# Two conversion calls after each of seven experts, raw tiles asked for at a call's end, and a branch that is announced

## The chip, the cores and the metric

The program runs on one core of a Trainium2 chip. The core has a tensor engine (PE, with its weight load PEld), a vector engine (DVE), a scalar engine (ACT), GpSimd (POOL), and SP, which mostly issues transfers. Each engine works through its own list of instructions in order; semaphores hold an instruction until what it needs is done, and whatever stands behind it on that engine waits too. The metric is the device time of one execution in microseconds (us): the median of several runs.

## The reference

Three blocks follow each other, on 2304 tokens of 512 values.

```
attn_out = _attn_ref(**attn_kwargs)            # 4 batches, 8 heads, 576 tokens, 64 values a head
x = _moe_ref(x=x, **moe_kwargs)                # 8 experts, each token goes to one or none
return _moe2_ref(x=x, **moe2_kwargs)           # gated block over all tokens

# _moe_ref, for each expert e
h = np.maximum(xc[mask] @ w1[e], 0.0)          # 512 -> 1024
y[mask] = gate_w[mask, None] * (h @ w2[e])     # 1024 -> 512
# _moe2_ref
gate = 1.0 / (1.0 + np.exp(-(x @ w_gate)))     # 512 -> 1536
return (gate * (x @ w_val) @ w_out)            # 1536 -> 512
```

The weights of the last block come as float64 and are turned into pairs of float32 (a high and a low part) on the chip.

## The kernel before

Attention takes the first 150 us or so. Then come the experts, then the gated block (`moe2_phase`) in six passes over five blocks of tokens, then a loop for tokens that found no place in an expert (`Overflow.run`). How many rounds that loop makes is known on the chip only; with these inputs it makes none. From the experts on, everything stands in `tc.manual_schedule()`: each engine keeps the order in which the code is written.

**One expert** (`moe_phase`) has four chunks. A chunk is `products1` on PE (L1165) into one of three banks, then ACT's `hh` (L1210) and DVE's `hl` (L1211), which empty the bank, then `wt.split`, which splits a chunk of the second weight into high and low (ACT L927, DVE `w_lo` L928), then `feed()`, which asks for more expert weights on SP's queue (L918). After the chunks come the turning of the next expert's tokens (`make_xt`, ACT L1105), some calls of `cv.tick()`, the second products for slots 128 to 255 (`second_half`), for slots 0 to 127 (`products2`, L933 to L935), the weighted sum (`add_up`, DVE) and the scatter back to memory (POOL). How many calls an expert has stands in `TICKS`.

**The conversion** (`Convert`, `cv`) turns 36 raw tiles of 512 KB into high and low parts, in six stages, each on an engine of its own:

- l: SP asks for a raw tile (L997). Three raw buffers, so tile i waits for b of tile i-3.
- a: ACT takes the absolute value of the high word (L1002).
- b: ACT takes its sign (L1040), DVE puts the bits together in three instructions (L1042, L1043, L1046).
- c: POOL multiplies by the sign (L1007).
- h: ACT rounds to the high part (L1014).
- o: DVE subtracts for the low part (L1017).

One call of `tick()` lets each stage go on by one tile, as far as the stage ahead of it was asked for. Nothing in a call waits; its instructions wait, on the engines, in the places where the calls put them.

```
def tick(self):
    for stage in "lohcba":
        self.go(stage)
```

Of the kernel before, what the change touches and what calls it, by code (L numbers as in the profile page):

```python
# [23 lines left out]
NJ = 5  # L24
CAP = 256
NEG = -1.0e30


class Attention:
# [48 lines left out]
    def setup(self):  # L78
# [8 lines left out]
        gp.affine_select(  # L87
            out=r, in_=r, pattern=[[0, 4], [1, 2 * W]], compare_op=ALU.is_ge, fill=NEG,
            base=-1, channel_multiplier=-1,
        )  # L90
        gp.affine_select(
            out=r, in_=r, pattern=[[0, 4], [-1, 2 * W]], compare_op=ALU.is_ge, fill=NEG,
            base=W, channel_multiplier=1,
# [14 lines left out]
        ve.tensor_copy(mp, m0)  # L108
        ve.memset(mp[0:32, :, 0:W], NEG)
        ve.tensor_copy(md, m0)  # L110
        ve.memset(md[:, :, 0:W], NEG)
        for h2 in range(2):
# [839 lines left out]
class Convert:  # L952
# [95 lines left out]
        )  # L1048

    def tick(self):  # L1050
        for stage in "lohcba":
            self.go(stage)

    def need(self, c, k):
# [3 lines left out]
def moe_phase(nc, tc, ctx, g, wt, pool_a, na, route, xd, cv, over, new_xt):  # L1058
# [1 line left out]

    TICKS = (0, 2, 3, 3, 3, 2, 2, 0)
    pool_b = ctx.enter_context(tc.tile_pool(name="m_w", bufs=1, reuse_waits="tile"))
    px = ctx.enter_context(tc.tile_pool(name="m_x", bufs=3, reuse_waits="tile"))
    p = ctx.enter_context(tc.tile_pool(name="m_p", bufs=2, reuse_waits="tile"))
# [30 lines left out]
    def make_xt(e):  # L1097
        xt = p.tile([128, 4, CAP], F32, tag="xt", name="xt")

        def turn(h):  # L1100
            for k in range(4):
                nc.tensor.transpose(xts[h][:, k], xg[e, h][:, 128 * k:128 * k + 128], g.ident)

        turn(0)
        nc.scalar.copy(out=xt[:, :, 0:128], in_=xts[0])  # L1105
        if e == 0:
            load_n(0)
        with tc.If(taken[e] > 128) as c:
            turn(1)
        with c.Else():  # L1110
            nc.tensor.matmul(xts[1][:, 0, 0:32], lhsT=g.one, rhs=g.one[:, 0:32], start=True, stop=True)
        nc.vector.tensor_copy(xt[:, :, 128:256], xts[1])
        return xt
# [89 lines left out]
    for e in range(E):  # L1203
        hs = []
        for c in range(4):
# [6 lines left out]
                out=lo, in0=ps, scalar=0.0, in1=hi.bitcast(F32), op0=ALU.max, op1=ALU.subtract  # L1212
# [7 lines left out]
            if c == 0 and e == E - 1:  # L1220
# [6 lines left out]
                for h in range(2):  # L1227
                    nc.gpsimd.tensor_scalar(
                        out=hot[:, h], in0=route.iota, scalar1=to[:, h:h + 1], scalar2=None, op0=ALU.is_equal
# [3 lines left out]
        if e + 1 < E:  # L1233
            xt = make_xt(e + 1)
        for _ in range(TICKS[e]):
            cv.tick()
# [62 lines left out]
def moe2_phase(nc, tc, ctx, g, cv, xt0, begun, acc, xd, out):  # L1299
# [79 lines left out]
    def sums_of(q, b, parts):  # L1379
        return [lambda a=a, t=t: s2(q, a, t, parts) for a, t in enumerate(tiles[b])]  # L1380

    def flush(left=0):
        while len(due) > left:
            due.pop(0)()
# [9 lines left out]
    for q in range(NP):  # L1394
# [3 lines left out]
        for b in order:  # L1398
# [13 lines left out]
                if q or b > 2:  # L1412
                    cv.tick()
            due += sums_of(q, b, parts)
    flush()


class Overflow:
# [163 lines left out]
def convert_sources(wg, wv, wo):  # L1582
    wg, wv, wo = (w.bitcast(I32) for w in (wg, wv, wo))
    srcs = []
    for i in range(FF // 256):
        for w in (wg, wv):
            for h in range(2):
                srcs.append(
                    w[256 * h:256 * h + 256, 512 * i:512 * i + 512].rearrange("(k p) f -> p k f", p=128)
                )  # L1590
        for h in range(2):
            srcs.append(
                wo[256 * i + 128 * h:256 * i + 128 * h + 128, :].rearrange("(k p) f -> p k f", p=128)
            )
    return srcs
# [26 lines left out]
@with_exitstack  # L1622
def fused_kernel(ctx: ExitStack, tc: tile.TileContext, q, k, v, w_skip, w_gate, w1, w2, wg, wv, wo, out):
    nc = tc.nc
    g = Globals()
    g.nc = nc
    const = ctx.enter_context(tc.tile_pool(name="const", bufs=1))
    dram = ctx.enter_context(tc.tile_pool(name="dram", bufs=1, space=DRAM))
    g.ident = const.tile([128, 128], F32, name="ident")
    make_identity(nc, g.ident)  # L1630
    xd = dram.tile([NT, DM], F32, name="xd")
    route = Route(nc, tc, ctx, g)
    g.one = route.one
    nc.vector.memset(g.one, 1.0)
    over = Overflow(nc, tc, ctx, g, route)
    na = 4
    pool_a = None
    cv = Convert(nc, convert_sources(wg, wv, wo))
    with tc.manual_schedule(), ExitStack() as right, ExitStack() as ctx_ps:
        with ExitStack() as c3:  # L1640
            wt = Weights(nc, tc, c3, w1, w2)
            with ExitStack() as c2:
                route.enter(c2)
                att = Attention(nc, tc, c2, g, q, k, v, w_skip, w_gate, xd)

                def extra(s):


                    nonlocal pool_a
                    if s == EXTRA:  # L1650
                        att.nat_ctx.close()
                        pool_a = ctx.enter_context(tc.tile_pool(name="w_a", bufs=na, side="right"))
                        wt.pool_x = pool_a
                    if s is None or s in LOADS:
                        n = wt.n1 + wt.n2
                        wt.load(2 if n < 18 and n // 4 % 2 else 1)

                attention_phase(att, route, extra)
                g.keep_busy(att.ps_t, "t", "ps_t", 5)
                route.finish_gates()  # L1660
            cv.enter(tc, right)
            pool_x = right.enter_context(tc.tile_pool(name="f_x", bufs=1, side="right"))
            with ExitStack() as c2:
                g.banks(ctx_ps.enter_context(tc.tile_pool(name="banks", bufs=1, space=PSUM, reuse_waits="tile")))
                over.enter(c2, g.spare)
                new_xt = lambda: tuple(
                    pool_x.tile([128, 4, 256], F32R, tag="xt" + n, name="fx" + n) for n in ("h", "l")
                )
                xt0, begun = moe_phase(nc, tc, c2, g, wt, pool_a, na, route, xd, cv, over, new_xt)
        with ExitStack() as c2:  # L1670
            pool_o = c2.enter_context(tc.tile_pool(name="f_o", bufs=1, reuse_waits="tile"))
            acc = [pool_o.tile([128, DM], F32, name=f"fo{t}") for t in range(NT // 128)]
            moe2_phase(nc, tc, c2, g, cv, xt0, begun, acc, xd, out)
    n = over.rounds()
    with ExitStack() as c2:
        over.run(n, c2, xd, w1, w2, cv, out)


# [27 lines left out]
```

## Time and profile before

| | us |
|---|---|
| three runs | 784.02, 778.4, 781.0 |
| median | 781.0 |
| profiled execution, its own time | 783.18 |
| its span in the profile | 781.5 |

Times of stretches below are counted in the span of the profiled execution. Its own time lies 1.7 us above its span and 2.2 us above the median of the three runs. The experts e0 to e6 end, for PE, at 169.5, 188.9, 211.1, 231.0, 252.1, 271.8 and 293.1 us; expert 7 and the start of the gated block run to 311, the gated block to 773.5, and the rest is the end of the program. PEclk is the clock granted to PE, 1.00 for 2.4 GHz and 0.50 for 1.2 GHz.

### The profile page before, as it was taken

To read this page: it belongs to the slowest core of one execution; us is meant where nothing else is said; L and a number is where in the kernel's file an instruction comes from. 1 tells how busy PE (TensorE), PEld (TensorE's weight loads), DVE (VectorE), ACT (ScalarE), POOL (GpSimd) and SP (SyncE) were. 2 spreads that over 40 slices of the span, in tenths; PEclk is the share of its full clock that TensorE was granted. 3 is DMA by queue.
4 is the path that set the end of the run, shared out by engine and by line. 5 is a ranking of instruction groups with operands and counts; after the bars stand their busy time and mean duration, and the time that the engine had idled before them with its cause. 6 is when DMAs were issued, how large, how long until landed. Compare 5 with 4: busy or idle time off the path is not lost.

```text
span 781.5 us, 13025 instructions
## 1 busy us (share of the span) xinstructions
PE 733.2 (94%) x4976; PEld 594.7 (76%) x4976; DVE 419.9 (54%) x880; ACT 306.9 (39%) x677; POOL 141.3 (18%) x163
## 2 busy tenths in 40 slices
PE   5999988779999779999999999999999999999995
PEld 3666665568988778978888888888888888888884
DVE  8767767556777757332234546534652653332332
ACT  4888884234545544333352323313321331111110
POOL 7224332312343233100011002000110010000000
PEclk9999999899999989999999999999999999999999
DMA  8799879595597762321012103100310000000122
GB/s 151 166 211 218 226 168 309 162 348 199 184 332 255 264 231 65 117 81 55 1 32 76 28 27 96 40 27 22 87 28 27 28 1 0 1 1 27 55 81 85
DMA packets 74997, 88.12 MB, mean 113 GB/s; under 512 B 15810, under 2 KB 52930, under 8 KB 74912
## 3 DMA queue, kind: packets, MB, share of 16 engines
q1 hardware_dynamic: 71008, 78.68, 34.9%
q0 software_dynamic: 2560, 6.15, 2.2%
q10 hardware_dynamic: 1344, 2.10, 0.7%
q8 instruction: 60, 0.98, 0.5%
q14 instruction: 25, 0.20, 0.1%
HBM read 75.52 MB, written 13.63 MB: 114 GB/s over the span
## 4 chain that ended last, share of the span: by engine, by line
PE 78%; DVE 7%; ACT 6%; DMA 5%; issue 3%; POOL 0%; SPq 0%; DVEq 0%; ACTq 0%; POOLq 0%
PE bank L942 26%; PE bank L947 13%; PE bank L935 8%; PE bank L933 8%; PE bank L934 8%; PE bank L1165 6%; DMA cv_raw<-in_moe_w_val_dram 2%; DMA cv_raw<-in_moe_w_gate_dram 2%; DVE w_lo L928 1%; ACT qTd L242 1%; PE ps_s L260 1%; ACT kTp L242 1%; ACT kTd L242 1%; PE ps_t L383 1%; DVE hl L1211 1%
## 5 line engine op out<-in xcount | busy, mean ns | idle before, releaser
L942 PE MATMUL bank<-fxh,w_hi 128*128 128x512 f32 (+1 forms) x480 | 177.7, 376 | 0.7 <-ACT fxh L1333 0.7
L942 PE MATMUL bank<-fxh,w_lo 128*128 128x512 f32 (+1 forms) x480 | 174.7, 370 | 0.0
L1359 DVE SCALAR_TENSOR_TENSOR th<-th,bank 128x512 f32<-128x512 f32 (+1 forms) x60 | 38.0, 634 | 184.3 <-PE bank L947 161.8
L947 PE MATMUL bank<-fxl,w_hi 128*128 128x512 f32 (+1 forms) x480 | 121.2, 372 | 0.0
L942 PEld LDWEIGHTS bank<-fxh,w_hi 128*128 128x128 f32 x480 | 90.3, 188 | 19.7 <-ACT fxh L1333 1.3
L1007 POOL TENSOR_TENSOR cv_x<-cv_x,cv_s 128x512 f32<-128x512 f32 x36 | 47.6, 1326 | 307.5 <-DVE cv_x L1046 282.2
L942 PEld LDWEIGHTS bank<-fxh,w_lo 128*128 128x128 f32 x480 | 90.3, 188 | 16.1
L947 PEld LDWEIGHTS bank<-fxl,w_hi 128*128 128x128 f32 x480 | 85.6, 188 | 17.5
L1165 PE MATMUL bank<-xt,w 128*128 128x128 f32 (+3 forms) x512 | 74.6, 309 | 16.6 <-issue 9.4
L1360 ACT CAST gh<-th 128x512 fp32r<-128x512 f32 (+1 forms) x60 | 34.7, 578 | 135.3 <-DVE th L1359 135.3
L1165 PEld LDWEIGHTS bank<-xt,w 128*128 128x128 f32 x512 | 71.8, 210 | 19.4 <-issue 9.6
L933 PE MATMUL bank<-w_hi,gh 128*128 128x512 f32 x216 | 85.6, 396 | 0.0
L934 PE MATMUL bank<-w_lo,gh 128*128 128x512 f32 x216 | 85.2, 395 | 0.0
L935 PE MATMUL bank<-w_hi,gl 128*128 128x512 f32 x216 | 85.2, 394 | 0.0
L1358 ACT ACTIVATE th<-bank 128x512 f32<-128x512 f32 (+1 forms) x60 | 33.3, 555 | 127.3 <-PE bank L947 126.8
L1375 DVE SCALAR_TENSOR_TENSOR fo<-bank,fo 128x512 f32<-128x512 f32 x90 | 61.6, 687 | 5.1 <-PE bank L935 3.0
L1361 DVE TENSOR_TENSOR gl<-th,gh 128x512 fp32r<-128x512 f32 (+1 forms) x60 | 39.2, 653 | 38.6 <-ACT gh L1360 38.6
L935 PEld LDWEIGHTS bank<-w_hi,gl 128*128 128x128 f32 x216 | 40.5, 188 | 9.6
L933 PEld LDWEIGHTS bank<-w_hi,gh 128*128 128x128 f32 x216 | 40.7, 188 | 9.2
L934 PEld LDWEIGHTS bank<-w_lo,gh 128*128 128x128 f32 x216 | 40.6, 188 | 9.1
L1002 ACT ACTIVATE cv_x<-cv_raw 128x512 f32<-128x512 f32 x36 | 24.2, 674 | 57.4 <-issue 32.8
L928 DVE TENSOR_TENSOR w_lo<-w,w_hi 128x1024 fp32r<-128x1024 f32 x32 | 41.3, 1292 | 3.7 <-ACT w_hi L927 3.4
(215 smaller groups left out, 1052.8 us busy)
## 6 DMA issues: line engine op xcount, KB each, us to landing
w<-in_moe_w_dram SPq DMA_DIRECT2D x62, 512.0 KB, 6.7
cv_raw<-in_moe_w_val_dram SPq DMA_DIRECT2D x12, 512.0 KB
cv_raw<-in_moe_w_out_dram SPq DMA_DIRECT2D x12, 512.0 KB, 7.1
cv_raw<-in_moe_w_gate_dram SPq DMA_DIRECT2D x10, 512.0 KB, 3.9
out_dram<-fo SPq DMA_DIRECT2D x18, 256.0 KB, 2.0
fx<-xd SPq DMA_DIRECT2D x16, 256.0 KB, 3.0
kp<-in_k_dram SPq DMA_DIRECT2D x12, 192.0 KB, 4.1
qp<-in_q_dram SPq DMA_DIRECT2D x12, 192.0 KB, 5.2
```

The lines of the kernel that those rows point to most:

```text
L928: self.nc.vector.tensor_tensor(out=lo, in0=raw, in1=hi.bitcast(F32), op=ALU.subtract)
L933: nc.tensor.matmul(out, lhsT=lh[0], rhs=rh[0], start=first, stop=False)
L934: nc.tensor.matmul(out, lhsT=lh[0], rhs=rh[1], start=False, stop=False)
L935: nc.tensor.matmul(out, lhsT=lh[1], rhs=rh[0], start=False, stop=last)
L942: nc.tensor.matmul(out, lhsT=lh[a][:, k], rhs=rh[0][:, k], start=first and k + a == k0, stop=False, skip_group_check=True,)
L947: nc.tensor.matmul(out, lhsT=lh[0][:, k], rhs=rh[1][:, k], start=False, stop=last and k == k1 - 1, skip_group_check=True)
L1007: nc.gpsimd.tensor_tensor(out=self.x[i], in0=self.x[i], in1=self.s.pop(i), op=ALU.mult)
L1165: nc.tensor.matmul(ps[:, a, 0:n], lhsT=wt.one[4 * e + c][:, k, 128 * a:128 * a + 128], rhs=xt[:, k, 0:n], start=(k == 0), stop=(k == 3),)
L1359: nc.vector.scalar_tensor_tensor(out=th, in0=th, scalar=1.0, in1=ps[1], op0=ALU.add, op1=ALU.mult)
L1360: nc.scalar.copy(out=hi, in_=th)
L1361: nc.vector.tensor_tensor(out=lo, in0=th, in1=hi.bitcast(F32), op=ALU.subtract)
L1375: nc.vector.scalar_tensor_tensor(out=o, in0=ps, scalar=0.5, in1=o, op0=ALU.mult, op1=ALU.add)
```

## The change

Four things are changed. In a call of `tick()` the stage l comes last instead of first. `TICKS` gives each of the first seven experts two calls (14 in all) where they had 0, 2, 3, 3, 3, 2 and 2 (15). The number of overflow rounds is loaded onto the engines ahead of the gated block instead of behind it. And the overflow loop stands inside a branch that is skipped as a whole when there are no rounds; a hint ahead of the last sums announces that branch to all five engines.

```diff
+ENGINES = [getattr(mybir.EngineType, e) for e in ("PE", "DVE", "Activation", "Pool", "SP")]
...
     def tick(self):
-        for stage in "lohcba":
+        for stage in "ohcbal":
             self.go(stage)
...
-    TICKS = (0, 2, 3, 3, 3, 2, 2, 0)
+    TICKS = (2, 2, 2, 2, 2, 2, 2, 0)
...
-    flush()
+    with tc.block():
+        tc.mark_branch_hint_location("over", "LikelyTaken", ENGINES)
+        flush()
...
+            n = over.rounds()
             moe2_phase(nc, tc, c2, g, cv, xt0, begun, acc, xd, out)
-    n = over.rounds()
-    with ExitStack() as c2:
-        over.run(n, c2, xd, w1, w2, cv, out)
+    with tc.If(n > 0, label="over"):
+        with ExitStack() as c2:
+            over.run(n, c2, xd, w1, w2, cv, out)
```

Line numbers of the changed kernel are one higher from `Convert` on. In the lists below, `bank_` with a number is a bank of PE's results and `cv_raw`, `cv_x`, `cv_s` are the conversion's tiles.

ACT between the turned tokens of expert 5 and the first chunk of expert 5, that is the calls at the end of expert 4, before:

```order
L1014 CAST w_hi<-cv_x 128x512
L1040 ACTIVATE cv_s<-cv_raw 128x512
L1180 UNCONDITIONAL_BRANCH
L1002 ACTIVATE cv_x<-cv_raw 128x512
L1014 CAST w_hi<-cv_x 128x512
L1040 ACTIVATE cv_s<-cv_raw 128x512
L1123 UNCONDITIONAL_BRANCH x3
L1002 ACTIVATE cv_x<-cv_raw 128x512
L1014 CAST w_hi<-cv_x 128x512
L1040 ACTIVATE cv_s<-cv_raw 128x512
L1002 ACTIVATE cv_x<-cv_raw 128x512
L1210 ACTIVATE hh<-bank_2977 128x512
```

ACT in the same place, after:

```order
L1106 COPY xt<-bank_2973 128x4x128
L1015 CAST w_hi<-cv_x 128x512
L1041 ACTIVATE cv_s<-cv_raw 128x512
L1181 UNCONDITIONAL_BRANCH
L1003 ACTIVATE cv_x<-cv_raw 128x512
L1015 CAST w_hi<-cv_x 128x512
L1041 ACTIVATE cv_s<-cv_raw 128x512
L1003 ACTIVATE cv_x<-cv_raw 128x512
L1124 UNCONDITIONAL_BRANCH x3
L1211 ACTIVATE hh<-bank_2977 128x512
```

One round of three instructions has gone from between the turned tokens and the next expert's first `hh`.

SP at the end of expert 0 and the beginning of expert 1 (`w_` with a number is an expert's weight chunk), before:

```order
L918 DMA w_3214<-in_moe_w_dram 128x4x256
L918 DMA w_3216<-in_moe_w_dram 128x2x512
L918 DMA w_3270<-in_moe_w_dram 128x4x256
L918 DMA w_3272<-in_moe_w_dram 128x2x512
L918 DMA w_3405<-in_moe_w_dram 128x4x256
L918 DMA w_3407<-in_moe_w_dram 128x2x512
```

SP in the same place, after:

```order
L919 DMA w_3214<-in_moe_w_dram 128x4x256
L919 DMA w_3216<-in_moe_w_dram 128x2x512
L919 DMA w_3270<-in_moe_w_dram 128x4x256
L919 DMA w_3272<-in_moe_w_dram 128x2x512
L998 DMA cv_raw<-in_moe_w_val_dram 128x2x512
L1181 UNCONDITIONAL_BRANCH
L998 DMA cv_raw<-in_moe_w_val_dram 128x2x512
L919 DMA w_3418<-in_moe_w_dram 128x4x256
L919 DMA w_3420<-in_moe_w_dram 128x2x512
```

Raw tiles 2 and 3 are now asked for ahead of expert 1's weight loads; each expert's two requests stand one expert earlier than the instructions that use them.

POOL from the last scatter of the experts to the loop, before:

```order
L1092 DMA xd<-xg,r_dst 2304x512 x2
L1007 TENSOR_TENSOR cv_x<-cv_x,cv_s 128x512 x23
L1479 TENSOR_LOAD v_n
L1488 COMPARE_AND_BRANCH
L1488 ISA
L1488 UNCONDITIONAL_BRANCH
```

POOL in the same place, after:

```order
L1093 DMA xd<-xg,r_dst 2304x512 x2
L1482 TENSOR_LOAD v_n
L1008 TENSOR_TENSOR cv_x<-cv_x,cv_s 128x512 x24
L1416 UNCONDITIONAL_BRANCH
L1706 BRANCH_PREFETCH_HINT
L1416 UNCONDITIONAL_BRANCH
L1678 COMPARE_AND_BRANCH
L1491 COMPARE_AND_BRANCH
```

The load of the number of rounds stands ahead of the gated block's products, the hint behind them, and a comparison of its own ahead of the loop's.

## Rows read from the trace of the kernel before

**Rows 1.** The page: the span, and the chain that ended last by engine.

```profile
span 781.5 us, 13025 instructions
...
PE 78%; DVE 7%; ACT 6%; DMA 5%; issue 3%; POOL 0%; SPq 0%; DVEq 0%; ACTq 0%; POOLq 0%
```

**Rows 2.** Busy time by stretch: an expert, and the gated block.

```profile
core 0: us, PE busy (x) PEld busy (x) DVE busy (x) ACT busy (x) POOL busy (x), PEclk, DMA share, GB/s
...
252.10:271.80 19.70, 15.36 (x95) 13.94 (x94) 14.09 (x21) 11.59 (x18) 6.41 (x5) 0.91 0.75 262
...
311.00:773.50 462.50, 461.79 (x2158) 378.96 (x2156) 194.93 (x321) 127.14 (x226) 30.67 (x24) 1.00 0.13 42
```

**Rows 3.** What PE waited for from 231 to 302: total, times, longest (us).

```profile
PE bank L1165 <- DVE hl L1211: 7.0, 4, 3.8
PE bank L1165 <- issue: 3.5, 3, 2.0
```

**Rows 4.** What ACT waited for from 231 to 302.

```profile
ACT w_hi L1014 <- POOL cv_x L1007: 11.8, 2, 6.5
ACT cv_x L1002 <- DMA cv_raw<-in_moe_w_gate_dram: 10.6, 2, 6.0
...
ACT cv_x L1002 <- DMA cv_raw<-in_moe_w_val_dram: 3.7, 1, 3.7
```

**Rows 5.** ACT in order of time, end of expert 4: start, duration, [idle before].

```profile
257.96 0.68 ACT L1002 ACTIVATE cv_x<-cv_raw 128x512 f32<-128x512 f32 x1 [3.67 <-DMA cv_raw<-in_moe_w_val_dram]
...
260.16 0.63 ACT L1210 ACTIVATE hh<-bank 128x512 fp32r<-128x512 f32 x1
```

**Rows 6.** PE in order of time, first chunks of experts 5 and 6.

```profile
262.26 0.49 PE L1165 MATMUL bank<-xt,w 128*128 128x128 f32 x2 [3.81 <-DVE hl L1211]
...
283.57 0.80 PE L1165 MATMUL bank<-xt,w 128*128 128x128 f32 x2 [1.22 <-DVE hl L1211]
```

**Rows 7.** Busy time by stretch, columns of rows 2: three stretches of 3.3 us.

```profile
263.10:266.40 3.30, 3.30 (x18) 3.24 (x18) 3.30 (x5) 2.50 (x5) 1.58 (x1) 0.50 0.58 171
276.80:280.10 3.30, 3.30 (x18) 3.30 (x17) 0.00 (x0) 0.19 (x1) 0.19 (x1) 0.50 1.02 376
283.60:286.90 3.30, 3.30 (x15) 3.30 (x16) 3.14 (x4) 2.99 (x5) 0.98 (x1) 0.50 0.24 47
```

**Rows 8.** The raw tiles: b's last step (ns, min/median/max), and requests from issue to landing.

```profile
L1046 DVE SCALAR_TENSOR_TENSOR cv_x<-cv_raw,cv_x x36: 691/693/2275, 186.7 to 636.5; 128x512 int32<-128x512 int32 x36
...
DMA to landing us min/median/max: 3.2/3.9/11.1
```

**Rows 9.** PE's sequencer at the branch ahead of a chunk of expert 5 (ns).

```profile
L1123 PEldq COMPARE_BRANCH  x1: 2710/2710/2710, 256.3 to 256.3; - x1
```

**Rows 10.** DVE and POOL in order of time, early in expert 6.

```profile
285.50 1.22 DVE L928 TENSOR_TENSOR w_lo<-w,w_hi 128x1024 fp32r<-128x1024 f32 x1
...
287.24 2.78 DVE L928 TENSOR_TENSOR w_lo<-w,w_hi 128x1024 fp32r<-128x1024 f32 x1
...
287.59 1.33 POOL L1007 TENSOR_TENSOR cv_x<-cv_x,cv_s 128x512 f32<-128x512 f32 x1
```

**Rows 11.** SP's last loads for expert 7, and ACT's last split there.

```profile
285.01 2.10 SPq L918 DMA_DIRECT2D w<-in_moe_w_dram  x2
...
299.25 1.04 ACT L927 CAST w_hi<-w 128x1024 fp32r<-128x1024 f32 x1
```

**Rows 12.** The number of rounds, PE's load of it (ns).

```profile
L1479 PEldq TENSOR_LOAD <-v_n x1: 375/375/375, 771.5 to 771.5; - x1
```

**Rows 13.** The end of the program, by sequencer (q): duration in ns, first and last start.

```profile
L1488 PEldq COMPARE_BRANCH  x2: 181/1828/3475, 773.7 to 778.5; - x2
L1488 POOLq COMPARE_BRANCH  x1: 33/33/33, 777.6 to 777.6; - x1
...
L1702 SPq DRAIN  x3: 7/7/7, 778.9 to 780.7; - x3
...
L1702 POOLq DRAIN  x2: 103/1395/2687, 777.8 to 780.7; - x2
```

## The prediction

> **What bounds the kernel now.** I began with the page. The chain that ended last is PE's for 78% of the 781.5 us, with DVE, ACT and DMA far behind [rows 1]; so a gain has to be a time in which PE stands still or runs slowly, or lie behind PE's last product. The busy times by stretch then say where such time is. In the gated block PE is busy for 461.79 of 462.50 us at full clock [rows 2]: nothing that the change does there can give more than 0.7 us, and the one product and one vector step more that move into its first pass lie on POOL (30.67 us busy) and DVE (194.93), which have room. Expert 5 is another matter: 15.36 of 19.70 us, at a mean clock of 0.91 [rows 2].
>
> The list of PE's waits from 231 to 302 us names them: 7.0 us in four waits for `hl`, the DVE step that empties a bank of the first products, and 3.5 us in three of "issue" [rows 3]. The same list for ACT says what is behind it: ACT waits for raw tiles that are still on their way (10.6 us in two, 3.7 in one) and for POOL's product (11.8 in two) [rows 4]. The view in order of time shows the link at one place. At the end of expert 4 ACT sits 3.67 us ahead of a `cv_x` whose raw tile has not landed, at 257.96, does the rest of the call, and only at 260.16 begins the `hh` of expert 5's first chunk [rows 5]; `hl` follows that, and PE, which has three banks and has filled them, stands 3.81 us until 262.26 [rows 6]. The same goes on at 283.57 with 1.22 us [rows 6]; the other two of the four waits make up the 2.0 us left.
>
> A second cost stands behind the first. In the 3.3 us from 263.1 and again from 283.6 PE is busy throughout at a granted clock of 0.50, that is 1.2 GHz [rows 7]; ahead of them it had stood still 3.81 and 1.22 us. Such a stretch would take half as long at 2.4 GHz, so each costs 1.65 us, 3.3 together. A third one at 276.8 [rows 7] follows an "issue" wait of 2.0 us, the longest of that kind [rows 3], which the change doesn't touch, and stays.
>
> **The requests for raw tiles.** With l last in a call and two calls to an expert, tile k is asked for two calls ahead of its stage a, where it was one. As the calls of one expert stand together on ACT, one call ahead means that the request and its use can fall into the same microseconds; two ahead means that a whole expert lies between. The shortest of experts 1 to 6 lasts 19.4 us, by the ends in the table. From issue to landing a raw tile took 3.9 us in the median and 11.1 at most [rows 8], so all the ACT waits for raw tiles go (14.3 us of ACT's time [rows 4]); POOL's products come earlier with them, and so does what ACT waits for from POOL. ACT then is through with its calls before PE has its first bank, and the 7.0 us of `hl` waits go, and with them the two slow stretches.
>
> Three things stay of these 10.3 us. First, at 256.3 PE's sequencer spends 2.71 us in a branch [rows 9], to 259.0; the products that it had issued ended at 258.45 (3.81 ahead of 262.26). So 0.6 us of the 3.81 wait come back as "issue". Second, DVE has 14.09 us of work in expert 5's 19.70 [rows 2], of which the conversion is a part that doesn't leave; at the boundaries into experts 6 and 7 `hl` may still come a little late. The bounds are nothing and all that the waits other than the long one had, 3.2 us; I take 1.0, since it is ACT's lateness, in the rows, that made `hl` late. Third, the second slow stretch may stay for the "issue" waits around it: 0 to 1.65, taken at 0, since the first and third stretch both followed an `hl` wait by under 1 us.
>
> **The calls.** Expert 0 gets two calls where it had none. Two raw tiles more are asked for while expert weights load; 1 MB at the 376 GB/s that the queues reached [rows 7] is 2.8 us of transfers. It is on the path only if PE runs out of expert 1's weights, which are asked for an expert ahead, so I take nothing. The third calls of experts 2, 3 and 4 go, and with them three of ACT's instructions per expert from the place where `hh` waits (0.68, 0.62 and 0.68 us [rows 5]); that is part of the 7.0. The last expert's b and c of one tile move into the gated block, at nothing, by the room named above.
>
> **The number of rounds.** The loads of it move from the end to the start of the gated block. PE's took 0.375 us [rows 12]; ahead of the gated block PE has work to do, so it may cost 0 to 0.4, and I take 0.2. DVE, ACT and POOL have waits of their own there.
>
> **The end.** Behind PE's last product come 8.0 us (773.5 to 781.5). POOL is let out of the empty loop's last step at 777.6 and then spends 2.69 us in a DRAIN, from 777.8 to 780.5, while SP, which has to wait for the last output to land, has its own first DRAIN at 778.9 [rows 13]. So POOL's DRAIN is the last of the chain, by 1.6 us. With the loop stepped over as a whole, POOL reaches its DRAIN without waiting for the loop's exit, and long before. SP's chain is then the last one, and is a little shorter for the steps that are left out of it: 1.7 us less. The bounds: 2.0, if SP's part shrinks more, and -0.4, if each of the two new branches makes an engine fetch code as PE does now (3.475 us in a branch from 773.7 [rows 13]): one such fetch more would end at about 780.6, with barrier and drains behind it 781.8 or so. I take 1.7, because PE's time in that branch is over by 777.2, before SP is through.
>
> The Trainium skill ("Runtime: NRT & Kernel Launch", section "Instruction fetch mechanics") says that a taken branch whose target lies outside what an engine holds stalls it for a fetch; by that rule the stepped-over loop costs PE a fetch like the one in the trace, and no more than that one. The trace agrees as far as 2.71 and 3.475 us in branches go.
>
> **The sum.** 7.0 + 3.3 - 0.6 - 1.0 - 0.2 = 8.5 us in the experts, 1.7 at the end: 10.2. The profiled execution of 783.2 would be 773.0; it lies 2.2 above the median of the three runs, so against that median the forecast is 781.0 - 10.2 = 770.8 us. That is 1.3% faster; 1%, or 7.8 us, is about what a measurement of this kernel can tell from no change.
>
> **Rivals.**
>
> DVE and POOL take the place (0.2). Each of the seven experts now ends with two POOL products, close together and all on time, where before some fell into ACT's waits. In expert 6 a `w_lo` of 2.78 us, against 1.22 for the one before, lay over a POOL product of 1.33 [rows 10]: 1.56 us more. If one such step falls ahead of the first `hl` at each of the four boundaries, 6.2 us of the 10.3 come back in place of the 1.0: 10.3 - 0.6 - 0.2 - 6.2 = 3.3, with the end 5.0, and 776.0 us. For it: DVE is the engine with least room in rows 2 behind PE. Against it: the step may as well fall behind the first `hl`, where three banks cover it. The Trainium skill ("SBUF — State Buffer", section "Who interferes with whom") says that a DVE instruction with two inputs in SBUF and a GpSimd instruction that reads SBUF exclude each other for a whole instruction, as those two in rows 10 have; the trace agrees with 1.56 us for 1.33.
>
> The announcement and the branch bring nothing (0.1): POOL's 2.69 us DRAIN is there whenever POOL ends, or a fetch takes its place. Then 8.5 are left, and 772.5.
>
> More than forecast (0.1): no DVE lag and no third slow stretch either (its 1.65), which makes 10.3 + 1.65 - 0.6 - 0.2 + 1.7 = 12.85, and 768.2.
>
> The change doesn't do what it says (0.05): SP works in order too, and a raw tile's request waits behind an expert's weight loads whose buffers are not free; if it leaves SP as late as now, only the end's gain and the fewer calls are left, and it is about 779.
>
> Slower (0.05): a request for tile k+3 now stands on SP behind stage b of tile k in the same call, and the next expert's eight weight loads stand behind it. If SP is held until b is done, each of six experts' loads start later by a and b of a tile: 0.68 for `cv_x`, as much for the sign, and three steps of DVE at no more than the 0.69 of the last [rows 8], 3.4 us. Without slack 20.6 us of PE waits come in where 10.2 go: 791.4 us. It decides only where SP's loads have less than 3.4 us to spare. The tightest that I found, expert 7's last two, were issued from 285.0 on and split by ACT at 299.25 at the latest [rows 11], so with a landing like that of a raw tile some 10 us are to spare.
>
> **How the numbers follow.** The forecast has 0.5. Within 1% lie the DVE rival and the one in which nothing moves, a small part of the forecast's own spread and of the announcement's: 0.31. Faster by over 1%: 0.64. Slower by over 1%: 0.05. The range goes down to the best ends of all terms (768.2, with 2.0 at the end 767.9) less 1.5 us for a median of runs that spread over 5.6, rounded to 766, and up past the DVE rival by as much, and by the end's gain, to 779.
>
> **What would show it.** Right: from 231 to 302 no wait of ACT for raw tiles and none of PE for `hl` over 1 us; clock 1.00 behind the boundary into expert 5; a stretch of experts 5 and 6 shorter by some 6 us; POOL's DRAIN far ahead of the end, and some 6.3 us from PE's last product to the end instead of 8.0. The DVE rival shows as `hl` waits that end with a `w_lo` of over 2 us. Wrong would make it a new "issue" wait of PE in the experts: all code behind the changed calls lies elsewhere, and the sequencer's branches can cost more or less than the 3.5 us they do now, which I could not price and leave inside the range.

## The result, and the profile after

The changed kernel takes 774.65 us (median of 20 runs) where the kernel before takes 781.04 in as many: 0.9916 of it, with a 95% interval of 0.9896 to 0.9936, that is 5 to 8 us. The forecast was 770.8, and 766 to 779 as its range; the sign and the range held, and the size was 6.4 us instead of 10.2. One execution in all that follows, among the twelve of the number of calls alone, took 1775.58 us, and the ratio given there leaves it out.

The profiled execution fell by 8.4 us, from a span of 781.5 [rows 1] to this one on the page after:

```profile
span 773.1 us, 12965 instructions
```

Not all of that is the change. PE's first product of expert 0 started at 150.68 us before and at 146.75 after, in code that is the same in both; over the fourteen profiled kernels of this case, all with the same attention, it starts between 146.4 and 152.5. So the stages are read by their own lengths. From that product to the first of expert 7 it was 142.4 us before and 138.0 after. From there to PE's last product it was 480.4 and 481.8, and from that to the end 8.0 and 6.6.

The list of what PE waited for, from 231 to 302 us, is the one to set beside [rows 3]; it is total, times and longest:

```profile
PE bank L1166 <- DVE hl L1212: 5.2, 3, 2.5
PE bank L1166 <- issue: 2.9, 1, 2.9
PE bank L935 <- DVE w_lo L929: 1.0, 1, 1.0
```

The waits for `hl` have not gone: 5.2 us of 7.0 are there, and 3.4 in a second profile of the same kernel, so that one profile tells such a sum to within some 2 us. ACT's list for the same stretch shows what became of [rows 4]:

```profile
ACT w_hi L1015 <- POOL cv_x L1008: 18.7, 2, 9.6
```

The 14.3 us for raw tiles have no row any more, as foretold; the wait for POOL's product has grown from 11.8 to 18.7 (12.0 in the second profile). In order of time, POOL, ACT and PE at the start of expert 6, and PE's one wait at that of expert 7 (start, duration, [idle before]; the three views are set one under the other):

```profile
260.99 1.00 POOL L1093 DMA_INDIRECT xd<-xg,r_dst  x1 [4.58 <-DVE w_lo L929]
268.52 1.05 POOL L1085 DMA_INDIRECT xg<-xd,r_src  x1 [6.53 <-DMA xd<-xg,r_dst]
...
270.91 2.50 POOL L1008 TENSOR_TENSOR cv_x<-cv_x,cv_s 128x512 f32<-128x512 f32 x2
```

```profile
272.22 0.62 ACT L1015 CAST w_hi<-cv_x 128x512 fp32r<-128x512 f32 x1 [9.58 <-POOL cv_x L1008]
...
273.86 0.57 ACT L1211 ACTIVATE hh<-bank 128x512 fp32r<-128x512 f32 x1
```

```profile
275.21 2.05 PE L1166 MATMUL bank<-xt,w 128*128 128x128 f32 x16 [2.51 <-DVE hl L1212]
...
292.51 0.71 PE L1166 MATMUL bank<-xt,w 128*128 128x128 f32 x4 [2.22 <-DVE hl L1212]
```

POOL issues a scatter at 260.99, and next in its list is the gather for expert e+2. That gather reads what the scatter writes, so it waits 6.53 us for the landing. The conversion's products stand behind the gather, ACT's rounding waits for the first of them, ACT's sign, absolute value and `hh` stand behind the rounding, and PE stands until 275.21. The raw tile is nowhere in this chain.

The wait at 292.51 has another end. DVE and POOL there, in order of time:

```profile
278.88 2.85 DVE L929 TENSOR_TENSOR w_lo<-w,w_hi 128x1024 fp32r<-128x1024 f32 x1
...
286.71 1.51 DVE L1043 TENSOR_SCALAR cv_x<-cv_x 128x512 f32<-128x512 f32 x1
...
289.32 1.41 DVE L1192 SCALAR_TENSOR_TENSOR xg<-bank,r_gslot,xg 128x512 f32<-128x512 f32 x2
290.64 1.22 DVE L929 TENSOR_TENSOR w_lo<-w,w_hi 128x1024 fp32r<-128x1024 f32 x1
291.77 0.69 DVE L1212 SCALAR_TENSOR_TENSOR hl<-bank,hh 128x512 fp32r<-128x512 f32 x1
```

```profile
279.32 1.32 POOL L1008 TENSOR_TENSOR cv_x<-cv_x,cv_s 128x512 f32<-128x512 f32 x1
286.35 1.57 POOL L1008 TENSOR_TENSOR cv_x<-cv_x,cv_s 128x512 f32<-128x512 f32 x1 [5.72 <-DVE cv_x L1047]
```

A conversion step that takes 0.42 us elsewhere takes 1.51 beside a POOL product, the rest of the call, two sums and a split stand ahead of `hl`, and it comes at 291.77. The `w_lo` of 278.88 had taken 2.85 us, against 1.22 elsewhere, over another POOL product, and the view shows DVE no idle time from there to `hl`: the two steps lost 1.6 and 1.1 us, and PE's wait is 2.22. That is the first rival's mechanism, in the place of one wait of three. The conversion step has one SBUF input, unlike the `w_lo` of [rows 10]; the Trainium skill ("SBUF — State Buffer", section "Who interferes with whom") has such steps contend with GpSimd when they run in a mode of two ports, and the trace fits that with 1.51 us against 0.42, without showing the mode.

From 231 to 302 us the clock gave what was counted on. Of the three stretches of 3.3 us at 1.2 GHz [rows 7] one is left, behind a wait of 2.92 us for "issue" (busy times by stretch, columns of rows 2):

```profile
267.20:270.40 3.20, 3.20 (x15) 3.20 (x16) 0.00 (x0) 0.00 (x0) 1.58 (x2) 0.50 0.89 314
```

The reason given does not hold, though. The slow stretches were to go with the waits for `hl`; two such waits of over 2 us stayed, and behind both the granted clock is 1.00, that is 2.4 GHz (from 275.2, and the same from 292.5):

```profile
275.20:278.50 3.30, 3.29 (x26) 3.15 (x27) 3.10 (x4) 3.30 (x6) 1.05 (x2) 1.00 0.58 185
```

Nor is it so in all stages. Experts 0 to 3, then 4 to 6, each from its first product on, before and after:

```profile
150.68:231.00 80.32, 73.40 (x435) 66.58 (x436) 55.28 (x77) 35.76 (x52) 25.52 (x20) 0.96 0.75 258
231.00:293.11 62.11, 52.95 (x306) 47.86 (x305) 42.03 (x62) 30.81 (x48) 21.07 (x17) 0.92 0.74 254
```

```profile
146.75:228.30 81.55, 74.82 (x434) 68.12 (x435) 54.03 (x85) 36.57 (x54) 22.05 (x20) 0.92 0.78 262
228.30:284.77 56.47, 49.50 (x306) 44.35 (x305) 37.80 (x50) 28.69 (x45) 19.67 (x16) 0.97 0.78 258
```

Experts 4 to 6 are 5.6 us shorter at a higher mean clock, experts 0 to 3 1.2 us longer at a lower one; over all seven the mean clock is 0.94 in both profiles.

At the end of the program the DRAIN of 2687 ns [rows 13] is gone from POOL (by sequencer, ns, first and last start):

```profile
L1706 SPq DRAIN  x3: 7/7/7, 772.3 to 772.6; - x3
...
L1706 POOLq DRAIN  x2: 45/79/113, 772.5 to 772.9; - x2
...
L1678 SPq EVENT_SEMAPHORE  x8: 17/17/17, 769.6 to 771.4; - x8
...
L1678 PEldq COMPARE_BRANCH  x1: 3110/3110/3110, 764.5 to 764.5; - x1
```

PE's long branch starts at 764.5, ahead of its last product, and is over by 767.7, while SP, which has the last output to wait for, waits up to 771.4.

### The profile page after: what moved, and what is told of

Its sections match the earlier page's. It is cut to its first block, busy times and chain, and to the rows that moved or that the text cites. A ratio compares the mean times of both kernels' runs of the same rounds, so it can differ in the third digit from the quotient of the medians.

```text
span 773.1 us, 12965 instructions
## 1 busy us (share of the span) xinstructions
PE 729.6 (94%) x4976; PEld 591.5 (77%) x4976; DVE 414.0 (54%) x880; ACT 306.6 (40%) x677; POOL 139.5 (18%) x163
## 4 chain that ended last, share of the span: by engine, by line
PE 79%; ACT 7%; DVE 5%; DMA 4%; issue 3%; POOL 1%; SPq 0%; POOLq 0%; DVEq 0%; ACTq 0%
PE bank L943 26%; PE bank L948 13%; PE bank L934 8%; PE bank L936 8%; PE bank L935 8%; PE bank L1166 6%; DMA xd<-xg,r_dst 2%; ACT qTd L243 2%; ACT kTp L243 2%; DMA xg<-xd,r_src 1%; ACT kTd L243 1%; PE ps_t L384 1%; PE ps_s L261 1%; ACT qTp L243 1%; ACT p L275 1%
## 5 line engine op out<-in xcount | busy, mean ns | idle before, releaser
L943 PEld LDWEIGHTS bank<-fxh,w_hi 128*128 128x128 f32 x480 | 90.3, 188 | 19.7 <-ACT fxh L1334 1.3
L1166 PE MATMUL bank<-xt,w 128*128 128x128 f32 (+3 forms) x512 | 72.5, 305 | 15.2 <-issue 10.0
L1166 PEld LDWEIGHTS bank<-xt,w 128*128 128x128 f32 x512 | 70.6, 208 | 17.3 <-issue 10.3
```

Source lines behind the costliest of these rows:

```text
L943: nc.tensor.matmul(out, lhsT=lh[a][:, k], rhs=rh[0][:, k], start=first and k + a == k0, stop=False, skip_group_check=True,)
L1166: nc.tensor.matmul(ps[:, a, 0:n], lhsT=wt.one[4 * e + c][:, k, 128 * a:128 * a + 128], rhs=xt[:, k, 0:n], start=(k == 0), stop=(k == 3),)
```

## The experiments

All ratios are to the kernel before, measured beside each version on the same chip, with 95% intervals; they need not be the quotient of the two medians. Theory 1 was the prediction's: what counts is how long ahead of its use a raw tile is asked for. Theory 2 was that the number of calls counts.

**The order of stages alone.**

```diff
-        for stage in "lohcba":
+        for stage in "ohcbal":
```

> The kernel before with l last in a call, and nothing else (15 calls, as before). Theory 1, the distance between a raw tile's request and its use is what counts: with two calls to an expert the use stands an expert later, but where an expert has three calls (e2, e3, e4) its third call uses what its first asked for, so ACT still waits for raw tiles at those boundaries and not at those into e6 and e7. That gives some 2 to 4 us of the change's 6.4: about 777 to 779. Theory 2, the number of calls is what counts: nothing, 781. The end stays at 8.0 us from PE's last product.

Measured: 779.47, 0.9995 (0.9965 to 1.0025). ACT's and PE's waits from 231 to 302:

```profile
ACT w_hi L1014 <- POOL cv_x L1007: 17.3, 2, 8.9
...
ACT cv_x L1002 <- DMA cv_raw<-in_moe_w_gate_dram: 1.0, 1, 1.0
```

```profile
PE bank L1165 <- DVE hl L1211: 6.9, 4, 3.0
```

The raw tiles are on time, 1.0 us instead of 14.3, even for three calls, and PE's 7.0 us of waits are 6.9. Theory 1 falls here. At the place of [rows 5], POOL and then ACT:

```profile
249.35 1.05 POOL L1084 DMA_INDIRECT xg<-xd,r_src  x1 [7.26 <-DMA xd<-xg,r_dst]
...
251.75 4.19 POOL L1007 TENSOR_TENSOR cv_x<-cv_x,cv_s 128x512 f32<-128x512 f32 x3
```

```profile
253.06 0.62 ACT L1014 CAST w_hi<-cv_x 128x512 fp32r<-128x512 f32 x1 [8.40 <-POOL cv_x L1007]
```

It is the scatter, gather, product chain again. In the kernel before, ACT was held twice at this place, by POOL's product up to 253.11 and by the raw tile up to 257.96 [rows 5]:

```profile
253.11 0.62 ACT L1014 CAST w_hi<-cv_x 128x512 fp32r<-128x512 f32 x1 [6.47 <-POOL cv_x L1007]
```

Without the second wait `hh` starts 6.2 us behind expert 5's first product (at 250.2) instead of 8.0 (at 252.1), though what ACT waits for from POOL now comes 2.9 us behind it instead of 1.0. Then DVE is late: ACT's `hh` and DVE's `hl` of the first chunk:

```profile
256.40 0.57 ACT L1210 ACTIVATE hh<-bank 128x512 fp32r<-128x512 f32 x1
```

```profile
258.65 0.68 DVE L1211 SCALAR_TENSOR_TENSOR hl<-bank,hh 128x512 fp32r<-128x512 f32 x1
```

The rest of the call and two sums stand ahead of `hl` on DVE. PE's longest wait is 3.0 us instead of 3.8: the raw tile ended last at this place, and what stands beside it ends nearly as late.

**The number of calls alone.**

```diff
-    TICKS = (0, 2, 3, 3, 3, 2, 2, 0)
+    TICKS = (2, 2, 2, 2, 2, 2, 2, 0)
```

> The kernel before with two calls for each of seven experts, and nothing else (l first in a call). Theory 1: a tile is asked for one call ahead of its use, so ACT goes on waiting for raw tiles at the boundaries, and the time is 779 to 782. Theory 2: the experts take as long as in the changed kernel, and only the end's 1.5 us are missing: about 776.

Measured: 777.32, 0.9961 (0.9937 to 0.9984), nearer to theory 2's 776 than to theory 1's 779 to 782. PE waits 3.4 us for `hl` from 231 to 302, and ACT goes on waiting for raw tiles:

```profile
PE bank L1165 <- DVE hl L1211: 3.4, 3, 2.2
```

```profile
ACT cv_x L1002 <- DMA cv_raw<-in_moe_w_val_dram: 7.9, 1, 7.9
ACT cv_x L1002 <- DMA cv_raw<-in_moe_w_gate_dram: 6.7, 1, 6.7
ACT cv_x L1002 <- DMA cv_raw<-in_moe_w_out_dram: 5.2, 1, 5.2
```

19.8 us of waits for raw tiles, more than before, and less of PE's time lost. What is missing on ACT's and POOL's path is the third call, with three ACT instructions ahead of `hh` and a POOL product behind the gather; moving the gather, below, takes the second away and leaves the first. Expert 5 took 15.0 us instead of 19.7.

**Both edits to the conversion, the old end.** The kernel before with the two diffs above.

> The kernel before with both edits to the conversion and none to the end. Both theories: the changed kernel's experts, no wait of ACT for raw tiles, and 1.5 us at the end not gained: about 776, with 8.0 us from PE's last product to the span's end. If the end's edits gave more than the profile shows, 778 or more.

Measured: 776.54, 0.9948 (0.9923 to 0.9973), 8.1 us from PE's last product to the end. ACT waits for no raw tile from 231 to 302, and PE still waits 6.9 us for `hl` there. Of the change's 6.4 us, 4.1 are the conversion's, with an interval of 2.1 to 6.0.

**The end alone.** The changed kernel with the old order and the old number of calls.

> The changed kernel with the old order of stages and the old number of calls, so that only the number of rounds, the branch and its hint are changed. From the profile after: 6.5 us from PE's last product to the end instead of 8.0, experts as before with 7 us of waits for hl: about 779.5. If the loads of the number ahead of the gated block cost PE something, PE's own time from the last expert to its last product is longer by up to 0.4.

Measured: 776.93, 0.9957 (0.9934 to 0.9980): 3.4 us, with an interval of 1.6 to 5.2, more than the 1.5 expected. Its profile has 6.3 us from PE's last product to the end, and 480.3 from the first of expert 7 to PE's last, as before. Together with the last experiment that is 0.95% where the whole change gives 0.84%: the two parts add up within their intervals.

**Without the hint.**

```diff
-    with tc.block():
-        tc.mark_branch_hint_location("over", "LikelyTaken", ENGINES)
-        flush()
+    flush()
```

> The changed kernel without the hint and its block, with the branch kept. If stepping over the loop as a whole is the gain at the end, 6.5 us from PE's last product to the end as in the changed kernel, give or take 0.2, since PE's fetch of code is over before the last output has landed. If the hint is what counts, 8.0 or more, with a branch of over 3 us on SP or POOL behind PE's last product.

Measured: 773.38, 0.9885 (0.9837 to 0.9933), no difference from the changed kernel that these runs could tell, with 5.9 us behind PE's last product. POOL's DRAINs there:

```profile
L1704 POOLq DRAIN  x2: 45/76/107, 772.1 to 772.5; - x2
```

So the branch around the loop is what shortens the end, and the announcement of it gives nothing that shows. In the eight profiles with the branch the end takes 4.9 to 6.6 us, on the mean 5.7; in the six without it 7.95 to 8.35, on the mean 8.1. That is 2.4 us.

**The gather behind the calls.** In the changed kernel:

```diff
-            if c == 3 and e + 2 < E:
-                gather(e + 2)
...
         for _ in range(TICKS[e]):
             cv.tick()
+        if e + 2 < E:
+            gather(e + 2)
```

> The changed kernel with the gather for expert e+2 behind the calls on POOL instead of ahead of them. Theory A, what is left of the waits for hl comes from POOL's order (a product of the conversion stands behind a gather that waits some 6.5 us for a scatter to land, ACT's rounding waits for the product, hh stands behind that): the waits of 0.5 and 2.5 us at the starts of experts 5 and 6 go, ACT waits no longer than 2 us for POOL there, and the time is 771 to 773. Theory B, DVE's own work makes hl late: the waits stay at some 5 us in all, and the time is as in the changed kernel, 774.7.

Measured: 771.93, 0.9876 (0.9841 to 0.9911). PE's waits from 231 to 302:

```profile
PE bank L1166 <- issue: 2.1, 2, 1.8
PE bank L1103 <- DMA xg<-xd,r_src: 2.1, 1, 2.1
PE bank L1166 <- DVE hl L1212: 1.8, 1, 1.8
```

Theory A holds for PE's waits: 5.2 us have become 1.8, and the one that is left is the one into expert 7. There ACT had stood 8.06 us for a POOL product that now stands behind a scatter. ACT's own waits for POOL did not fall under 2 us as expected: one of 5.10 us is left at the start of expert 6, but it ends before PE has run out of banks. Part of the gain comes back in a new place, 2.1 us for tokens that are now gathered later. The time is lower than the changed kernel's by 0.4%, with intervals that overlap.

**And one call of expert 6 after expert 7's chunks.**

```diff
-    TICKS = (2, 2, 2, 2, 2, 2, 2, 0)
+    TICKS = (2, 2, 2, 2, 2, 2, 1, 1)
```

> As the one before, and one of expert 6's two calls is made after expert 7's chunks (2, 2, 2, 2, 2, 2, 1, 1). In the changed kernel 2.2 us at the start of expert 7 go to an hl that stands on DVE behind a call's four steps (one of 1.5 us instead of 0.4, beside a POOL product) and two sums. Theory A for the rest and DVE's work here: that wait goes too, about 2 us less than the one before, 769 to 772. If the call only moves the wait to the end of expert 7, no difference.

Measured: 771.01, 0.9870 (0.9836 to 0.9905). From 231 to 302 PE has no wait for `hl` left in the list:

```profile
PE bank L1166 <- issue: 3.0, 3, 1.7
PE bank L1103 <- DMA xg<-xd,r_src: 2.4, 1, 2.4
PE bank L1133 <- DMA xo<-xd: 1.3, 2, 1.0
```

That it beats the version before it by the 2 us expected, the runs can't tell; it lost 1.3 us to old tokens that came late.

**The gather behind the calls, old order, 15 calls, old end; and the same with l last.** These two and `order_only` make a square with the kernel before.

> The kernel before, and only the gather for expert e+2 stands behind the calls on POOL. Theory A2, two chains of nearly the same length hold ACT up at the experts' ends, the raw tile's landing and POOL's product behind gather and scatter, so that either alone brings little: ACT still waits for raw tiles for over 10 us, PE for hl for 5 to 8 us, and the time is 778 to 781. Theory A1, POOL's order alone is the bound: the waits for hl go, 775 or less.

> The kernel before with l last in a call and the gather behind the calls, still 15 calls and the old end. Theory A2: with both chains gone the waits for hl at the starts of experts 4 to 6 fall to under 1 us each, some 4 to 6 us in the experts, though order_only brought nothing by itself: 774 to 777. If the number of calls is what counts, it stays at 779 to 781.

Measured: 777.58, 0.9962 (0.9939 to 0.9985), and 776.10, 0.9962 (0.9939 to 0.9984). PE's waits from 231 to 302 in the first, then ACT's for raw tiles:

```profile
PE bank L1102 <- DMA xg<-xd,r_src: 3.9, 1, 3.9
PE bank L1165 <- DMA w<-in_moe_w_dram: 2.4, 1, 2.4
...
PE bank L1165 <- DVE hl L1211: 1.6, 1, 1.6
```

```profile
ACT cv_x L1002 <- DMA cv_raw<-in_moe_w_val_dram: 2.8, 1, 2.8
```

One more wait for a raw tile, of 5.2 us, ended at 227.5, just ahead of this stretch. Moving the gather took the waits for `hl` from 7.0 to 1.6 with the old order, and to 0.6 with l last. So theory A2 (two chains of nearly equal length, both to be taken away) is not borne out: POOL's order was a bound, and the requests' order shows no effect in either row of the square (1.0000 and 0.9995 with the gather early, 0.9962 and 0.9962 with it late; the two medians of the late pair lie 1.5 us apart, less than such an interval spans). Theory A1 had the waits right and the time wrong: the total fell by 3.0 (1.2 to 4.8), not by 5 or more. In the profile more than the 5.4 us came back, 3.9 as tokens gathered late and 2.4 as an expert weight; 1.9 us less of "issue" and two slow stretches in place of three make up for it there.

**Raw tiles asked for twice.**

```diff
             (queue or nc.sync).dma_start(out=t.rearrange("p (k f) -> p k f", k=self.srcs[i].shape[1]), in_=self.srcs[i])
+            if 2 <= i < 16:
+                (queue or nc.sync).dma_start(out=t.rearrange("p (k f) -> p k f", k=self.srcs[i].shape[1]), in_=self.srcs[i])
```

> The changed kernel with raw tiles 2 to 15 asked for twice, one request behind the other into the same tile: 14 times 512 KB more. Theory C, PE's sequencer fetches code over the same queues as the transfers, so its branches are long where the queues are full (5.1 us at the start of expert 1 and 5.0 at that of expert 6, with the queues busy all the time, 1.4 to 2.2 where they are busy for 0.4 of it): the branches and PE's waits for issue become longer, from 9.5 us in all to 12 to 16, and the time goes up by 3 to 8. Against it: branches as long as before and only ACT's or PE's waits for data added.

Measured: 793.64, 1.0176 (1.0130 to 1.0223). PE's waits and ACT's, from 143 to 306:

```profile
PE bank L1168 <- DVE hl L1214: 17.3, 3, 10.7
PE bank L1168 <- issue: 5.0, 5, 2.3
```

```profile
ACT cv_x L1005 <- DMA cv_raw<-in_moe_w_gate_dram: 13.4, 3, 8.9
ACT cv_x L1005 <- DMA cv_raw<-in_moe_w_out_dram: 6.4, 2, 5.6
```

Theory C is not borne out: the waits for "issue" are 5.0 us instead of the changed kernel's 10.0, not longer. Nor is it refuted. PE's branches of over 0.9 us came to 27.9 us in eleven, against 23.8 in eight and 24.6 in nine in the two profiles of the changed kernel, and the queues' share from 147 to 306 us rose only from 0.72 to 0.81. For the edit does a second thing: SP holds the second request until the first has landed, 91 us in 13 waits from 143 to 306, of which this row has five:

```profile
SPq L1000 <- DMA cv_raw<-in_moe_w_val_dram: 35.3, 5, 10.1
```

Whatever stands behind on SP is asked for later. So ACT's waits for raw tiles come back, and with them 17.3 us of PE's for `hl`: a late raw tile can bound this stage, as it ended last at [rows 5].

**The changed kernel and the best version once more, side by side.**

> The changed kernel once more, on the same chip as the others of this call: 0.9916 of the kernel before, 774 to 775. It is there to be compared with the next.

> The changed kernel with the gather behind the calls and one call of expert 6 made after expert 7's chunks, once more: 0.987 of the kernel before, 3 to 4 us less than the changed kernel. If the earlier difference was chance, as the changed kernel.

Measured: 772.22, 0.9900 (0.9864 to 0.9936), and 769.72, 0.9854 (0.9819 to 0.9889). The version with the late gather and the call moved to expert 7 is 1.3 to 1.5% faster than the kernel before in both of its runs, and lies 0.5% below the changed kernel, once beside it and once against its 20 runs. The intervals still overlap, so by how much it beats the changed kernel is open.

## Why the prediction was right or wrong

Sign and range were right; the forecast gain of 10.2 us was 6.4, with an interval of 5 to 8. One step failed, two terms put at nothing cost something, and the end, sized too small, made up for part of it; that the time fell inside the range is in part luck.

**The step that failed** is in the part on the requests: "POOL's products come earlier with them, and so does what ACT waits for from POOL", and from it that the 7.0 us of `hl` waits go. The rows showed both waits of ACT side by side, 14.3 us for raw tiles and 11.8 for POOL [rows 4], and I let the second hang on the first. It hangs on a scatter's landing and a gather that POOL has to issue ahead of the product: with raw tiles on time alone the wait for POOL grew to 17.3 us and PE's stayed at 6.9. In experts 4 to 6 a later gather or fewer calls, each without the new order, took PE's waits for `hl` from 5.7 us to 0 and 1.2. So the order of stages, the centre of the forecast, gave nothing that could be measured, alone or beside the late gather.

**What I put in a clause** as "part of the 7.0", the third calls that go from experts 2, 3 and 4, is what the conversion's gain came from: 3.0 us (1.2 to 4.9) by that edit alone, 4.1 (2.1 to 6.0) with the order, where I had 8.5.

**What I put at nothing** is most of the difference. Leaving out the doubled requests, five profiles have the gather early and 14 calls, and three have it early and 15. With 14, experts 4 to 6 take 52.1 to 56.5 us instead of 60.5 to 62.1, on the mean 6.6 less. But experts 0 to 3 take 81.6 to 82.7 instead of 79.6 to 80.6, 2.2 more, and from expert 7's first product to PE's last it is 481.2 to 482.8 instead of 480.3 to 481.0, 1.2 more. The prediction has the two calls of expert 0, and the steps that move behind expert 7, at no cost. Most of the last is the later `hl` into expert 7; how the calls lengthen experts 0 to 3 no run shows.

**The clock term** of 3.3 us for two slow stretches between 258 and 290 held in the profile, where one stretch of three is left, as said; it is the one behind the "issue" wait. It held without the reason given: two waits that were to take the stretches with them stayed. Over the eight profiles just named experts 4 to 6 have none or one such stretch with 14 calls and two or three with 15; what decides it no run shows. Experts 0 to 3, of which the forecast says nothing, ran at a lower mean clock after than before. "0.6 back as issue" at the start of expert 5 went as no such wait at all there, and 0.47 for `hl`.

**The end** was 1.7 and measured 2.4 by the profiles, 3.4 (1.6 to 5.2) by the times. The mechanism was the one given: POOL's DRAIN of 2.69 us is 0.1 once POOL doesn't leave an empty loop. It was undersized because SP's chain got shorter by more than the 0.1 us I took: SP's first DRAIN stands 5.35 to 5.75 us behind PE's last product in the six profiles with the old end, on the mean 5.5, and 4.0 to 5.7 with the branch, on the mean 4.7. Its lower bound, a second long branch of PE (a fetch of code, in the prediction's words), did not come: PE's branch now starts ahead of its last product's end.

**The number of rounds** ahead of the gated block cost nothing to be seen: with that edit and the old conversion, expert 7 and the gated block took 480.3 us against 480.4.

**The rivals.** That the announcement brings nothing is right for the hint and wrong for the branch around the loop, which is what the rival bet on. DVE's lateness is real into expert 7, 2.2 us instead of 1.3, but not at the other starts of the changed kernel; with the order alone it shows at expert 5's start too. SP held by b did not slow anything: PE waited for no expert weight in the changed kernel's experts.

**What is open** is the length of PE's branches in the experts. They came to 21.6 to 30.1 us over the fourteen profiles, changed from run to run at the same place (2.1 and 3.4 us for the same code at 165 us of the changed kernel), and no edit here changed them in a way that these profiles can tell. Expert 1 took 18.4 to 22.0 us with them. It wasn't tried to move code or transfers away from a branch.

## What to carry to other kernels

When an engine waits for two things in the same list, follow each to its own first cause before giving both to one edit; the one that is removed may have stood beside another that ends nearly as late. And read each stage by its own length over several profiles: what moved out of one may lengthen another. An in-order queue that mixes transfers which wait for each other with arithmetic that others wait for is the first place to look, and moving the arithmetic ahead of the waiting transfer is a cheap test. The end of a program is worth a look of its own: an empty loop's exit can hold one engine back until everything else is done.

## What the runs showed of the hardware

A loop of no rounds left POOL with a DRAIN of 2.69 us at the very end, the same 2687 ns in all six profiles with the old end, while a branch around that loop left DRAINs of 0.05 and 0.11 us. A scatter and a gather that follow each other through the same memory cost POOL 2.6 to 8.9 us of waiting per expert in the nine profiles with the gather early (6.5 and 7.3 in the rows shown). With it one round of two scatters, two gathers and two products took 21.2 us in the changed kernel (from the gather at 247.3 to that at 268.5), longer than the 13.9 us from expert 5's first product to expert 6's. And beside a GpSimd product a vector step of one input took 1.51 us instead of 0.42, one of two inputs 2.85 instead of 1.22.
